# An added term ahead of each reciprocal: linear attention and spectral mixing on one core

## Chip, cores and metric

The kernel runs on one core of a Trainium2 chip. The metric is the device time of one execution in microseconds. The kernel before has a median of 419.33 us over three runs (418.85, 419.33 and 419.35).

## What is computed

The inputs are q, k and v of shape (8, 8, 576, 64) and the weights w_r, w_i (64, 512, 512) and w_ch (512, 512), all in float32. Cut to what matters:

```python
q_p, k_p = phi(q), phi(k)                      # phi(x) = max(x, 0) + 1 for x > 0, exp(x) below
kv  = einsum('bhsd,bhse->bhde', k_p, v)
z   = sum(k_p, axis=2)
num = einsum('bhsd,bhde->bhse', q_p, kv)
den = einsum('bhsd,bhd->bhs', q_p, z)[..., None] + 1e-06
x   = (num / den), heads side by side          # (8, 576, 512)
X   = rfft(x, axis=1); the first 64 modes are mixed over d by w_r + i w_i; y = irfft
u   = x + y
out = u + max(u @ w_ch, 0)
```

Each denominator is a sum of 64 products of features, and the reference adds 1e-6 to it. The kernel before divides by the sum alone.

## The kernel before, in words

The work is in three stages, and the order of nearly every instruction on every engine is written out by hand: `pin` (line 98) keeps an instruction at its place in the program.

**Attention stage (lines 436 to 475).** A loop over the 8 batches. For each batch q, k and v are loaded two batches ahead by DMAs issued on POOL's queue (`load`, L185; they go from float32 to float16, and each kind has two buffers, so a load waits until the batch two before has been used). ACT takes exponents (`exps`, L205 and L208) and DVE makes the features of them (`features`, L220, L226, and the copy of v into vpad, L232). PE transposes q into a PSUM tile qTp (`turn_q`, L242), ACT copies it out (L249). PE sums k and v into kvp (`sum_kv`, L262); v is padded with a column of ones, so that a 65th column holds z; ACT copies that into kv_sb (L274).

Then `form_x` (lines 279 to 304) runs over 5 tiles of rows, four of 128 and a tail of 64. PE multiplies into a PSUM tile num of two banks (`num_matmuls`, L156): for each of 8 heads 64 columns of numerator and one of denominator. DVE takes the reciprocal of the 8 denominators of each row straight from PSUM into rd (L295) and multiplies (L298), which leaves float16 rows x16, or x16t for the tail. The tiles qTp, kvp, num and xp share three PSUM buffers under the tag "big", so PE can be at most three such tiles ahead.

Between the tiles PE transforms the batch before to frequencies (`transform`, xf, L421 and L426; ACT scales the result into xsp, L433 and L434), and puts the one before that in its place as input of the weights' products (`place_x`, xp, L389 and L400; DVE and ACT copy it into xt_c, L409 and L410). On DVE the features of batch b+1 stand ahead of `form_x` of batch b. PE, DVE and ACT each go through this order; what is ahead in an engine's order holds up what is behind.

**Product stage (`mode_pair`, lines 532 to 557).** The 64 modes are handled as 32 pairs. A pair's weights are two DMAs of 1 MB written (`w_load`, L109, one for w_r and one for w_i), also on POOL's queue. Five pairs are loaded during the attention stage, and behind them w_ch (L600). From pair 5 on there are two buffers, so that the load of pair p+2 is issued when the products of pair p (L502, tile P) have read theirs; pair 5 takes the buffer of pair 0. In each pair DVE prepares the next input xz (L512), and DVE or ACT copies P out (L517, L519); PE sorts the result into yt (L525).

Into the gaps of this stage a work list is spread, so many items per pair. Its first items are `attention_rows` (lines 762 to 792): the rows of attention are computed a second time, now in float32 for the final sum. PE multiplies qT by kv_diag into banks nw (L773, four banks in turn). For even batches the reciprocals rd of the attention stage are used again; for odd batches, whose rows lie on other partitions, DVE takes the reciprocals anew, 4 per row and half tile, into rdw (L784). DVE multiplies (L786). Later items add the inverse transform to these rows and multiply by w_ch.

**Tail.** After the last load, in pieces (L121), the last modes, the inverse transform, the rectifier and the stores (L951, L957) follow.

The lines that matter here:

```python
        nv = num[orow, :, 0:260].rearrange("p o (c n) -> p o c n", c=4)
        rden = rd_all[b][orow, jj]
        pin(nc.vector.reciprocal(out=rden, in_=nv[:, :, :, 64]))
```

Of the kernel before, what the change touches and what calls it, by code (L numbers as in the profile page):

```python
# [33 lines left out]
def kernel(  # L34
# [10 lines left out]
    nc = tc.nc  # L45
# [52 lines left out]
    pin = tc.keep_in_program_order  # L98
# [45 lines left out]
    def rows_of(jj: int, base: int = 0):  # L144

        if jj < NJJ:
            return slice(base + jj, base + 512, NJJ)
        return slice(512, S) if base == 0 else slice(0, base)

    def num_matmuls(num, orow, qT, kv_sb, cols, pinned=False):  # L150
        for hpp in range(2):
            for h2 in range(2):
                for hpo in range(2):
                    rows = slice(hpo * 64, hpo * 64 + 64)
                    c0 = (hpp * 2 + h2) * 65
                    mm = nc.tensor.matmul(  # L156
                        num[hpo][orow, c0 : c0 + 65], qT[rows, hpp, h2, cols], kv_sb[rows, hpp, h2, :]
                    )
                    if pinned:
                        pin(mm)  # L160
        return [n[orow, 0:260].rearrange("p (c n) -> p c n", c=4) for n in num]

    def q_view(t):
        return t.rearrange("p (c t s) -> p c t s", c=2, t=2)
# [114 lines left out]
    def form_x(b, jj):  # L279
        if jj == 0:  # L280
            x16s[b] = (
                sA.tile([128, 2 * NJ * Dh * 2], F16, tag="x16", bufs=2, name=f"x16_{b}")[
                    :, 0 : NJJ * D
                ].rearrange("p (j d) -> p j d", j=NJJ),
                sA.tile([128, D], F16, tag="x16t", bufs=2, name=f"x16t_{b}"),
            )
        tail = jj == NJJ
        orow = HALVES[b % 2] if tail else slice(0, 128)
        num = psA.tile([128, 2, 512], F32, tag="big", bufs=3, name=f"num{b}_{jj}")
        num_matmuls(  # L290
            [num[:, o] for o in range(2)], orow, q_view(qT_all[b]), kv_all[b], rows_of(jj), True
        )
        nv = num[orow, :, 0:260].rearrange("p o (c n) -> p o c n", c=4)
        rden = rd_all[b][orow, jj]
        pin(nc.vector.reciprocal(out=rden, in_=nv[:, :, :, 64]))  # L295
        dst = x16s[b][1][orow, :] if tail else x16s[b][0][:, jj, :]
        pin(
            nc.vector.tensor_tensor(  # L298
                out=dst.rearrange("p (o c d) -> p o c d", o=2, c=4),
                in0=nv[:, :, :, 0:64],  # L300
                in1=rden.unsqueeze(3).broadcast_to([64 if tail else 128, 2, 4, Dh]),
                op=ALU.mult,
            )
        )
# [139 lines left out]
    for b in range(B):  # L444
        if b + 2 < B:
            load(b + 2)
            if b % 2 == 1:
                w_next()
        turn_q(b, 0)
        turn_q(b, 1)  # L450
        if b == 0:
            fold_table()
        sum_kv(b)
        if b + 1 < B:
            for _ in features(b + 1):
                pass
        if b + 2 < B:
            exps(b + 2)
        for jj in range(NJJ + 1):
            form_x(b, jj)  # L460
            if b == 0 and jj == 0:
                make_place()
            if b > 1 and jj == 1:
                place_x(b - 2)
            if b > 0 and jj in (2, 3):
                transform(b - 1, jj - 2)
        if b > 0:
            transform(b - 1, 2)
            transform(b - 1, 3)
# [204 lines left out]
    def x_of(t: int):  # L674
        if t < B * NJJ:
            return x_main[t // NJJ][:, t % NJJ, :]
        i = t - B * NJJ
        return x_tail[i // 2][:, i % 2, :]
# [10 lines left out]
    def bank(name: str, shape=(128, D), dtype=F32):  # L689
        return psB.tile(list(shape), dtype, tag="bank", bufs=4, name=name)  # L690
# [64 lines left out]
    def parts_of(t: int):  # L755
        if t < B * NJJ:
            b, jj = divmod(t, NJJ)
            return [(b, jj, slice(0, 128))]
        p = t - B * NJJ
        return [(2 * p + h, NJJ, HALVES[h]) for h in range(2)]  # L760

    def attention_rows(t: int):

        num = [bank(f"nw{t}_{c}") for c in range(2)]
        x = x_of(t)
        for b, jj, orow in parts_of(t):
            qT = q_view(qT_all[b])
            rd = rd_all[b][orow, jj].rearrange("p o (c t) -> p c t o", c=2)
            xv = x[orow].rearrange("p (o c t d) -> p c t o d", o=2, c=2, t=2)
            for c in range(2):  # L770
                for h2 in range(2):
                    pin(
                        nc.tensor.matmul(  # L773
                            num[c][orow, h2 * 130 : h2 * 130 + 130],
                            qT[:, c, h2, rows_of(jj, BASE[b % 2])],
                            kv_diag[:, b, c, h2].rearrange("p o n -> p (o n)"),
                        )
                    )
            for c in range(2):
                nv = num[c][orow, 0:260].rearrange("p (t o n) -> p t o n", t=2, o=2)  # L780
                rden = rd[:, c]
                if b % 2 == 1:
                    rden = sW.tile([128, 2, 2], F32, tag="rdw", bufs=4, name=f"rdw{t}_{c}")[orow]
                    pin(nc.vector.reciprocal(out=rden, in_=nv[:, :, :, 64]))  # L784
                pin(
                    nc.vector.tensor_tensor(  # L786
                        out=xv[:, c],
                        in0=nv[:, :, :, 0:64],
                        in1=rden.unsqueeze(3).broadcast_to([orow.stop - orow.start, 2, 2, Dh]),
                        op=ALU.mult,  # L790
                    )
                )
# [231 lines left out]
    def first_rows(n: int):  # L1024
# [8 lines left out]

    rows_work = [inverse_rows, row_sets] + [lambda i=i: row_set(i) for i in range(1 + N_LEAD)]
    work[:0] = [lambda t=t: attention_rows(t) for t in tiles[:8]] + rows_work + [
        lambda t=t: attention_rows(t) for t in tiles[8:]
    ]
    share(
# [98 lines left out]
    def sums_of(n: int, tiles_of):  # L1137
        channels(n, tiles_of)
        add_inverse(n, 1, tiles_of)
        for i in tiles_of:  # L1140
# [6 lines left out]
            out=x_of(0), in0=accs[0][:, 0], scalar=0.0, in1=x_of(0), op0=ALU.max, op1=ALU.add  # L1147
# [51 lines left out]
```

## Time and profile before

| | |
|---|---|
| Median of three runs | 419.33 us |
| Profiled execution | 418.91 us |
| Its span, first to last instruction | 417.2 us |
| PE, DVE, ACT, POOL busy | 292.3, 240.1, 152.7, 65.0 us |
| DMA moved | 92.86 MB, of it 81.54 MB issued on POOL's queue |
| Reciprocals L295 | 40, 198 ns in the median, from 25.5 to 104.9 us |
| Multiplies L298 | 40, 691 ns, from 25.8 to 105.1 us |
| Reciprocals L784 | 40, 172 ns, from 146.5 to 229.2 us |
| First product P starts | 114.75 us |
| Last piece of weights read by PE | 385.7 us |

All times within the execution are microseconds from the start of the span. A line of a timeline reads: start, duration, engine, line of the code, operation, output tile, input tile with their shapes, count, and in brackets how long the engine had been idle before it and what ended that. In the page's part 2 a digit is the busy share of one fortieth of the span (10.4 us), in tenths. A table of stages has for each stretch its length, the busy time of PE, PE's weight loads, DVE, ACT and POOL with the number of instructions, then the granted clock of PE, the DMA engines' share and GB/s. A line of DMA issues has the size and the microseconds from issue to landing.

### The profile page before, as it was taken

Reading aid. Unit: us, or ns where it says so; the run is one execution under the profiler, and the core shown is the slowest. Engines: PE = TensorE matmul, PEld = TensorE weight load, DVE = VectorE, ACT = ScalarE, POOL = GpSimd, SP = SyncE. Lnnn points to the kernel's source line nnn. Section 1 sums busy time; section 2 is a strip of 40 time slices with the busy share of each in tenths; the row PEclk is TensorE's granted clock in tenths of the full one; section 3 lists DMA queues with packets and bytes.
Section 4 is the critical chain, followed back from the end, with each engine's and each line's share of the span. In section 5 each row is a group of like instructions: output and inputs, shape, how many; then the busy total and the mean of one; then the engine's idle time right before and its main releaser. Section 6 shows DMA issues by size and latency. Waiting matters only on the chain.

```text
span 417.2 us, 6991 instructions
## 1 busy us (share of the span) xinstructions
PE 292.3 (70%) x2890; PEld 158.1 (38%) x2890; DVE 240.1 (58%) x533; ACT 152.7 (37%) x226; POOL 65.0 (16%) x115
## 2 busy tenths in 40 slices
PE   0279998999674355444435686978786887999993
PEld 0167776777421122212222232424332322453431
DVE  3779899695447474355536453564545354532795
ACT  4667787855200001000000233334342432331682
POOL 6232424200020111111111111111111111130200
PEclk9999999579755655566665589899998888899998
DMA  8999999999999999999999999999999999999698
GB/s 217 211 211 214 210 222 203 221 222 213 217 217 212 220 209 222 218 211 222 211 220 217 212 222 209 220 218 213 222 209 220 217 214 222 209 217 186 210 401 346
DMA packets 16998, 92.86 MB, mean 223 GB/s; under 512 B 2503, under 2 KB 3224, under 8 KB 12808
## 3 DMA queue, kind: packets, MB, share of 16 engines
q0 software_dynamic: 13088, 81.54, 94.0%
q1 hardware_dynamic: 3878, 10.90, 6.9%
q8 instruction: 22, 0.36, 0.3%
q14 instruction: 10, 0.07, 0.0%
HBM read 163.66 MB, written 9.44 MB: 415 GB/s over the span
## 4 chain that ended last, share of the span: by engine, by line
DMA 58%; PE 22%; DVE 9%; ACT 4%; issue 3%; POOL 3%; ACTq 0%; POOLq 0%
DMA w<-in_moe_w_i_dram 52%; DMA k<-in_k_dram 7%; PE P L502 5%; PE kvp L262 4%; DVE x_main L969 4%; DVE x L298 2%; PE qTp L242 2%; PE xp L389 2%; POOL w L109 2%; PE xf L421 1%; PE zl L489 1%; PE z L862 1%; ACT qT L249 1%; PE num L156 1%; PE acc L896 1%
## 5 line engine op out<-in xcount | busy, mean ns | idle before, releaser
L502 PE MATMUL P<-w,xz 128*32 128x512 bf16 x496 | 49.5, 540 | 70.8 <-DMA w<-in_moe_w_i_dram 68.5
L109 POOL DMA_DIRECT2D w<-in_moe_w_r_dram x31 | 17.3, 560 | 249.6 <-PE P L502 245.1
L519 ACT CAST ys<-P 128x512 f16<-128x512 f32 x15 | 8.8, 586 | 120.4 <-PE P L502 120.4
L502 PEld LDWEIGHTS <-xz 128*32 128x32 bf16 x496 | 13.6, 116 | 91.9 <-DMA w<-in_moe_w_i_dram 55.8
L517 DVE CAST ys<-P 128x512 f16<-128x512 f32 x17 | 11.8, 692 | 55.3 <-PE P L502 55.3
L842 PE MATMUL eps<-wch,xTw 128*128 128x512 f16 x144 | 41.1, 413 | 0.0
L825 ACT CAST x16w<-x_main 128x512 f16<-128x512 f32 x32 | 19.8, 618 | 37.0 <-DVE x_main L823 37.0
L823 DVE TENSOR_TENSOR x_main<-ya,x_main 128x512 f32<-128x512 f32 x32 | 22.0, 689 | 19.0 <-PE ya L819 18.8
L262 PE MATMUL kvp<-vpad,ke 32*128 32x130 f16 x576 | 23.8, 261 | 8.3 <-ACT qT L249 8.3
L773 PE MATMUL nw<-kv_diag,qT 128*128 128x130 f16 (+1 forms) x160 | 24.3, 294 | 6.6 <-DVE x_tail L786 3.2
L850 ACT CAST E<-eps 128x512 f16<-128x512 f32 (+1 forms) x40 | 21.2, 540 | 20.1 <-PE eps L842 20.1
L262 PEld LDWEIGHTS <-ke 32*128 32x128 f16 x576 | 21.9, 115 | 9.8 <-issue 9.2
L512 DVE COPY xz<-xt_c 64x256 bf16<-64x256 bf16 x62 | 22.9, 369 | 2.2 <-PE P L502 1.4
L298 DVE TENSOR_TENSOR x<-num,rd 128x512 f16<-128x512 f32 x32 | 22.1, 691 | 1.1
L242 PE MATMUL qTp<-id,qe 128*128 128x128 f16 x144 | 14.2, 277 | 11.4 <-DVE qe L226 9.7
L773 PEld LDWEIGHTS <-qT 128*128 128x128 f16 (+1 forms) x160 | 14.5, 134 | 20.0 <-issue 11.5
L834 DVE COPY xTw<-xTp 128x512 f16<-128x512 f16 x36 | 15.0, 416 | 10.5 <-PE xTp L832 10.4
L156 PE MATMUL num<-kv_sb,qT 64*128 64x65 f16 (+1 forms) x320 | 16.3, 218 | 6.3 <-DVE x L298 3.9
L249 ACT COPY qT<-qTp 128x1152 f16<-128x1152 f16 x16 | 19.6, 1289 | 2.1 <-PE qTp L242 2.0
L786 DVE TENSOR_TENSOR x_main<-nw,rd 128x256 f32<-128x256 f32 x32 | 11.2, 415 | 15.1 <-PE nw L773 15.1
L208 ACT ACTIVATE ke<-k 128x2304 f16<-128x2304 f16 x8 | 16.9, 2116 | 3.2 <-DMA k<-in_k_dram 3.2
L842 PEld LDWEIGHTS <-xTw 128*128 128x128 f16 x144 | 13.6, 106 | 11.6 <-issue 4.5
(153 smaller groups left out, 526.6 us busy)
## 6 DMA issues: line engine op xcount, KB each, us to landing
w<-in_moe_w_r_dram POOLq DMA_DIRECT2D x31, 1024.0 KB, 12.3
w<-in_moe_w_i_dram POOLq DMA_DIRECT2D x31, 1024.0 KB, 16.6
out_dram<-x_main SPq DMA_DIRECT2D x14, 512.0 KB, 3.4
v<-in_v_dram POOLq DMA_DIRECT2D x8, 576.0 KB, 14.2
q<-in_q_dram POOLq DMA_DIRECT2D x7, 576.0 KB, 12.5
k<-in_k_dram POOLq DMA_DIRECT2D x6, 576.0 KB, 12.5
q<-in_q_dram SPq DMA_DIRECT2D x2, 576.0 KB, 4.5
w<-in_moe_w_r_dram POOLq DMA_DIRECT2D x2, 512.0 KB, 11.2
```

The costliest lines, as they stand in the source:

```text
L109: nc.gpsimd.dma_start(out=w_in[p][half::2], in_=two.rearrange("g (r dc) e -> (g r) dc e", dc=NDW))
L156: mm = nc.tensor.matmul(num[hpo][orow, c0 : c0 + 65], qT[rows, hpp, h2, cols], kv_sb[rows, hpp, h2, :])
L242: nc.tensor.transpose(qT_ps[:, j], phi["q", b][:, c, j].rearrange("p o d -> p (o d)"), id16,)
L249: nc.scalar.copy(out=qT[:, :, c * NJ : (c + 1) * NJ], in_=qT_ps.rearrange("p j x -> p x j"))
L262: nc.tensor.matmul(kv_ps[:, h2, 0:130], phi["k", b][r0 : r0 + 32, j // NJ, j % NJ].rearrange("p o d -> p (o d)"), vp[r0 : r0 + 32, :, j, 0 ...
L298: nc.vector.tensor_tensor(out=dst.rearrange("p (o c d) -> p o c d", o=2, c=4), in0=nv[:, :, :, 0:64], in1=rden.unsqueeze(3).broadcast_to([ ...
L502: nc.tensor.matmul(P[c : c + n, :], x, w[:, dc, :], start=(dc < NDC), stop=(dc >= n_dc - NDC), tile_position=(0, c), skip_group_check=True,)
L512: pin(nc.vector.tensor_copy(out=xz[p % 2][HALVES[h], :, h, :], in_=src))
L773: nc.tensor.matmul(num[c][orow, h2 * 130 : h2 * 130 + 130], qT[:, c, h2, rows_of(jj, BASE[b % 2])], kv_diag[:, b, c, h2].rearrange("p o n ...
L823: pin(nc.vector.tensor_tensor(out=x, in0=acc, in1=x, op=ALU.add))
L842: nc.tensor.matmul(e_ps, xT[:, c, :], wch16[:, c, :], start=(c == 0), stop=(c == NDC - 1))
L850: pin(nc.scalar.copy(out=dst, in_=e_ps[:, cols]))
```

## The change

Ahead of each of the two reciprocals a `tensor_scalar_add` on the vector engine reads the denominators from PSUM, adds 1e-6 and writes them to the tile of the reciprocals; the reciprocal then works in place on that tile.

```diff
@@ form_x
         rden = rd_all[b][orow, jj]
-        pin(nc.vector.reciprocal(out=rden, in_=nv[:, :, :, 64]))
+        pin(nc.vector.tensor_scalar_add(out=rden, in0=nv[:, :, :, 64], scalar1=1e-6))
+        pin(nc.vector.reciprocal(out=rden, in_=rden))
@@ attention_rows
                 if b % 2 == 1:
                     rden = sW.tile([128, 2, 2], F32, tag="rdw", bufs=4, name=f"rdw{t}_{c}")[orow]
-                    pin(nc.vector.reciprocal(out=rden, in_=nv[:, :, :, 64]))
+                    pin(nc.vector.tensor_scalar_add(out=rden, in0=nv[:, :, :, 64], scalar1=1e-6))
+                    pin(nc.vector.reciprocal(out=rden, in_=rden))
```

## The prediction

> **What bounds the kernel now.** I read the page first. Its 40 slices show the DMA engines full from the first slice to near the end, and DVE at 7 to 9 tenths in the first ten slices; the chain gives DMA 58%.
>
> ```profile
> DVE  3779899695447474355536453564545354532795
> DMA  8999999999999999999999999999999999999698
> DMA 58%; PE 22%; DVE 9%; ACT 4%; issue 3%; POOL 3%; ACTq 0%; POOLq 0%
> ```
>
> So for 386 of 417 us the kernel is a stream of loads, and an edit to DVE counts only if it makes the stream run dry. The chain in order of time says where that can be. Up to 114.75 it mixes PE, DVE, ACT and one load; from 133 to 385 it is one load after another. The hand-over is between: the first product P (L502) waits for the last of the attention stage, and the load of pair 5 waits for that product. The POOL queue's timeline and the issues with their landing times, each asked for a stretch of its own, price it:
>
> ```profile
> 87.25 0.78 POOL L600 DMA_DIRECT2D wch<-in_moe_w_ch_dram  x1 [4.33 <-DMA w<-in_moe_w_r_dram]
> 116.95 0.52 POOL L109 DMA_DIRECT2D w<-in_moe_w_r_dram  x1 [28.92 <-PE P L502]
> ```
> ```profile
> wch<-in_moe_w_ch_dram POOLq DMA_DIRECT2D x1, 512.0 KB, 36.2
> ```
> ```profile
> w<-in_moe_w_r_dram POOLq DMA_DIRECT2D x1, 1024.0 KB, 11.4
> ```
>
> POOL stood idle 28.92 us for P. wch lands at 87.25+36.2 = 123.5. Pair 5's first half, issued at 116.95, lands at 128.35, 4.85 later, and 4.85 per half is the pace of all loads (their landings are spaced so). The stream was therefore not dry: there is a **cushion**. The packets say how much: the first of the 16 DMA engines is through with wch at about 121.25, the last at about 123.2, and the last small loads (row L1122) take about 1.1 us from issue to first packet; I use 1.3. An issue by 121.25-1.3 = 119.95 leaves no engine idle (cushion 3.0 us); by 123.2-1.3 = 121.9 the slowest engine alone is still covered (4.9 us). I take **3.0**, since past it engines stand idle, and keep 4.9 for the range.
>
> **What the change does to DVE.** The instruction order of the changed kernel has 80 more instructions, all on DVE: 40 adds at L295 and 40 at L784 (the latter for odd batches). Each add takes the wait for PE over; the reciprocal then waits for the add, as the multiply waits for the reciprocal. Nothing else moves; no DMA is added. The DVE timeline shows the unit into which an add goes:
>
> ```profile
> 28.49 0.20 DVE L295 RECIPROCAL rd<-num 128x8 f32<-128x8 f32 x1
> 28.72 0.69 DVE L298 TENSOR_TENSOR x<-num,rd 128x512 f16<-128x512 f32 x1
> 29.33 0.20 DVE L295 RECIPROCAL rd<-num 128x8 f32<-128x8 f32 x1
> ```
>
> From a reciprocal to the multiply that needs it is 0.23 us: 0.20 and 0.03 of waiting. No add of this shape is in the trace. The nearest above is the TENSOR_SCALAR of L355, from PSUM, 128x64 in 0.215; below, a MEMSET of one column in 0.06. With the 0.03 the add costs 0.09 to 0.25; below nothing is excluded, as an instruction is put into a chain and none is taken out. I take **0.235**, the pitch of the reciprocal, the row that it is nearest to (same tile, same kind of wait). The reciprocal now reads SBUF and not PSUM: I leave it at 0.20, within 0.03 either way (L741, SBUF, 128x16: 0.178).
>
> [...]
>
> **The attention stage (25 to 106 us): 40 tiles, 5 per batch, 5 x 0.235 = 1.2 us per batch.** I walk along the DVE timeline and take off every idle gap before it.
> - Batches 0 to 2: DVE is 1.2 later after each, and gets back what it had idle before vpad (0.33 at 35.67, 0.92 at 46.30) and before xt_c (0.63 at 49.59), as far as PE isn't late too. PE is, since num has 3 buffers and waits for the multiply before the last two. Left: 0.9, 1.15, then 1.75.
> - Batches 3 and 4 (52.8 to 77): DVE has no gap. 2.9, then 4.1; PE, which waits for x there already, 3.6.
> - At 73.82 PE's transposes of batch 5 had waited 1.20 us for ACT, which stood behind the load of k that landed at 71.04. That load was queued 13.3 us, so its landing doesn't move when its issue comes 1.8 later. Left: 3.6-1.2 = 2.4; DVE's 2.61 idle before 79.51 comes down to the same.
> - Batch 5: PE is the slower, DVE's gaps of 0.63 and 0.32 are used: 2.8. Batch 6: DVE 4.0, PE 3.3, and DVE's idle 4.12 before 100.79 brings it down to PE's:
>
> ```profile
> 96.13 1.18 PE L242 MATMUL qTp<-id,qe 128*128 128x128 f16 x18
> ```
> ```profile
> 100.79 0.21 DVE L295 RECIPROCAL rd<-num 128x8 f32<-128x8 f32 x1 [4.12 <-PE num L156]
> 105.11 0.69 DVE L298 TENSOR_TENSOR x16t<-num,rd 64x512 f16<-64x512 f32 x1
> ```
> - Batch 7: 3.3+1.15 = **4.4** at x16t, for which PE's xf already waits 0.32; then a chain of PE, DVE and ACT with no slack to P at 114.75.
>
> So of 9.4 us of adds 4.4 reach P. The issue at 116.95 becomes 121.35: 4.4-3.0 = **1.4 us of dry stream**, and from there the stream is a fixed train (9.7 us a pair), with a tail of 31.5 us after 385.7 that nothing touches. At the cheap end of the add (0.09) the walk gives some 1.7, inside the cushion; at 0.25 some 4.7, and 1.7 over.
>
> Earlier loads are covered: q of batch 7 is issued at 65.47, behind DVE's features of batch 5, now near 68.4; the stream has v of batch 6 until 73.7, less some 2 us of landing. What queues behind it on POOL (k, v, then eight halves of w) has more. If this cover went, its loss would come earlier and the cushion at 117 would grow by it.
>
> **The product stage (146 to 229 us): 40 adds more, 0.2 each, 8 us, costed at nothing.** P waits for its load, and after P the next issue has a whole pair in flight:
>
> ```profile
> 220.58 1.90 PE L502 MATMUL P<-w,xz 128*32 128x512 bf16 x16 [5.59 <-DMA w<-in_moe_w_i_dram]
> 230.27 1.90 PE L502 MATMUL P<-w,xz 128*32 128x512 bf16 x16 [2.15 <-DMA w<-in_moe_w_i_dram]
> ```
>
> The tightest pair has 10 of the 40 adds (224 to 229.8): PE's nw matmuls wait for DVE's banks, so P at 230.27 may lose up to 2.1 of its 2.15 us. Were it late, the next issue would have some 7 us before the stream is dry. If all this cover were gone, it would be up to 8 us.
>
> **Sum.** 418.91 (profiled execution; span 417.2 and 1.7 around it) + 1.4 = 420.3. The three runs have median 419.33, 0.4 above it; I give the median's figure, 419.33 + 1.4 = **420.7**. Runs differ by 0.5 us, so about 0.2% (0.84 us) is what can be told from no change.
>
> **Rivals.**
> - *The cushion holds: no change.* Mechanism: DMA engines that run dry for a moment don't matter as long as the slowest isn't, so the cushion is 4.9 and not 3.0; it decides from a delay of 4.9 us on. For it: w lands when its last engine does, and 4.4 is under 4.9; a cheaper add, 0.15, gives 2.8. Against: the mean rate over 16 engines has nothing spare. Time: 419.3 (419.0 to 420.1).
> - *PE loses clock: slower still.* The stages view:
>
> ```profile
> 60.00:70.00 10.00, 8.63 (x176) 6.87 (x175) 9.66 (x19) 7.80 (x11) 3.11 (x5) 1.00 1.01 199
> 70.00:80.00 10.00, 8.09 (x118) 6.82 (x117) 7.22 (x14) 7.29 (x11) 2.74 (x6) 0.59 1.13 216
> 90.00:95.00 5.00, 4.53 (x108) 3.69 (x100) 4.47 (x10) 1.87 (x6) 0.00 (x0) 1.00 0.99 210
> ```
> The third column from the end is the granted clock. It falls about 72, after PE waited for x several times at 68.8 to 71. A batch at low clock takes PE 12.9 us (73.82 to 86.72), at full clock 9.4 (86.72 to 96.13); DVE with the adds needs about 10.4. More waiting for x can drop the clock one batch sooner, at 12.9-10.4 = 2.5 us: 420.7+2.5 = 423.2. Against: at 59 to 62 a wait of 0.59 didn't drop it. [...]
> - *Faster.* A clock gained in batch 5 would make up delay, but the stream has no gap to give; 419.33 less over 0.84 has no mechanism beyond a shift of that clock.
> - *It doesn't do what it says* is excluded: the adds stand in the order.
>
> **Numbers.** Forecast (over the cushion by 0.9 to 3) 0.47; cushion holds 0.37; clock lost 0.11; faster 0.05. So slower 0.58, same 0.37, faster 0.05. The range runs from 419.0, within the holding case, to 423.3, the clock's case: some 0.17 is left out.
>
> **What would show it.** After: DVE's L295 twice per tile at a pitch near 0.235; P first at about 119.2 and not 114.75; POOL's issue at about 121.3; its landing at about 129.8, and not 128.35, with wch still at 123.5; product pairs again 9.7 apart; 31.5 us after the last load. The cushion's case shows P late and the landing unchanged. The clock's case shows four xf matmuls at 0.62 instead of 0.41 between 58 and 72 or 95 and 106. I am wrong in kind if k's landing moves or a product pair exceeds 9.7.

## The result, and the profile after

The changed kernel takes 423.74 us in the median of 10 runs (420.07 to 425.55), the kernel before 419.01 us (418.83 to 419.35, 10 runs beside them): a ratio of 1.009 (of the means), interval 1.0061 to 1.012. It is slower by 4.7 us where 1.4 was forecast. The ten times are not one cluster: four lie at 420.1 to 420.3, six at 423.7 to 425.6, and before shows nothing of the kind. The profiled execution is one of the upper six: 424.23 us with a span of 422.5, against 418.91 and 417.2. Ratios here are taken without executions over 1.5% above the fastest of the same kernel; that matters for three experiments, and stands there.

First the page of the changed kernel: DVE, the granted clock, the DMA engines and their rate in 40 slices, which are now 10.6 us each, then the engines' shares of the chain.

```profile
DVE  4769889896544784466555653463527262622794
PEclk9999998588665555555665589798989696899997
DMA  8999999999999999999999999999999999998697
GB/s 216 212 210 216 209 215 188 214 209 218 220 169 220 220 208 218 220 217 209 219 221 206 219 223 214 211 220 218 208 221 219 216 213 220 217 208 164 240 402 304
DMA 49%; PE 27%; DVE 12%; ACT 4%; issue 3%; POOL 3%; ACTq 0%; DVEq 0%; POOLq 0%
```

The busy shares of the DMA engines look as full as before, but their rate does not. The same row of before's page:

```profile
GB/s 217 211 211 214 210 222 203 221 222 213 217 217 212 220 209 222 218 211 222 211 220 217 212 222 209 220 218 213 222 209 220 217 214 222 209 217 186 210 401 346
```

Before had no slice under 203 GB/s among the first 36, now slice 7 (63 to 74 us) has 188 and slice 12 (116 to 127 us) has 169. The stream has run dry twice. The chain says the same from the other side: DMA has lost 9 points, PE has gained 5 and DVE 3.

Next DVE's timeline of the changed kernel, for the same unit as in the prediction:

```profile
28.92 0.15 DVE L295 TENSOR_SCALAR rd<-num 128x8 f32<-128x8 f32 x1
29.11 0.20 DVE L296 RECIPROCAL rd<-rd 128x8 f32<-128x8 f32 x1
29.34 0.69 DVE L299 TENSOR_TENSOR x<-num,rd 128x512 f16<-128x512 f32 x1
```

The add takes 0.154 us in the median (0.146 to 0.170) and its successor starts 0.19 after it. The reciprocal that now reads SBUF takes 203 ns, against 198 from PSUM. Then the hand-over, from the POOL queue's timeline and PE's:

```profile
70.54 0.71 POOL L185 DMA_DIRECT2D q<-in_q_dram  x1 [8.23 <-ACT kv_sb L274]
...
88.69 0.78 POOL L601 DMA_DIRECT2D wch<-in_moe_w_ch_dram  x1 [4.31 <-DMA w<-in_moe_w_r_dram]
123.50 0.52 POOL L109 DMA_DIRECT2D w<-in_moe_w_r_dram  x1 [34.04 <-PE P L503]
```
```profile
121.30 1.90 PE L503 MATMUL P<-w,xz 128*32 128x512 bf16 x16 [2.25 <-ACT xt_c L411]
```

P starts at 121.30 instead of 114.75, 6.55 us late, and POOL issues pair 5 at 123.50 instead of 116.95. The issues with their landing times, of wch and of pair 5's first half:

```profile
wch<-in_moe_w_ch_dram POOLq DMA_DIRECT2D x1, 512.0 KB, 36.3
```
```profile
w<-in_moe_w_r_dram POOLq DMA_DIRECT2D x1, 1024.0 KB, 7.8
```

Pair 5's half lands at 123.50 + 7.8 = 131.3, not 128.35: 2.95 late. wch lands at 124.99, not 123.45, so 1.5 of the 2.95 are older. They come from the first row of the POOL fence: q of batch 7 was issued at 70.54, not 65.47, and the rate of the stream fell (slice 7 above). The other 1.45 us are lost between 123 and 126.5.

Last, the granted clock by stages, third column from the end:

```profile
60.00:70.00 10.00, 9.74 (x177) 7.49 (x175) 8.65 (x21) 8.18 (x9) 0.89 (x2) 1.00 1.01 199
70.00:80.00 10.00, 9.05 (x112) 6.50 (x107) 9.56 (x23) 7.00 (x11) 6.09 (x9) 0.58 1.03 175
80.00:90.00 10.00, 9.79 (x158) 7.77 (x156) 7.94 (x19) 7.99 (x9) 1.86 (x3) 0.57 1.08 225
90.00:100.00 10.00, 9.14 (x163) 7.21 (x163) 9.56 (x21) 4.70 (x9) 0.00 (x0) 0.83 1.01 215
```

The 1.00 of the first row must be read with care: up to the first change that a trace records, 64.75 us here, this column and the page's digits show full clock, also where the matmuls tell of half. PE's transposes of a batch (L242, 18 of them) tell the clock by themselves: before's take 1.18 us at 96.13, where the stages grant 1.00, and 2.10 at 86.72, where they grant 0.50. PE's timelines of before and of the changed kernel, batch 3:

```profile
52.84 1.18 PE L242 MATMUL qTp<-id,qe 128*128 128x128 f16 x18
```
```profile
54.82 2.10 PE L242 MATMUL qTp<-id,qe 128*128 128x128 f16 x18
```

In the changed kernel the first rise is at 64.75; before it was at 51.4. Between 50 us and P, with the time before the first rise counted as half clock, the changed kernel's PE was at half clock for 44.0 us, before's for 23.8. Those 20 us are what the prediction did not have.

### The profile page after: what moved, and what is told of

The parts are those of the page before. It is cut to its first block, busy times and chain, and to the rows that moved or that the text cites. A ratio compares the mean times of both kernels' runs of the same rounds, so it can differ in the third digit from the quotient of the medians.

```text
span 422.5 us, 7071 instructions
## 1 busy us (share of the span) xinstructions
PE 301.8 (71%) x2890; PEld 163.5 (39%) x2890; DVE 253.0 (60%) x613; ACT 153.0 (36%) x226; POOL 65.0 (15%) x115
## 4 chain that ended last, share of the span: by engine, by line
DMA 49%; PE 27%; DVE 12%; ACT 4%; issue 3%; POOL 3%; ACTq 0%; DVEq 0%; POOLq 0%
DMA w<-in_moe_w_i_dram 46%; PE P L503 6%; PE kvp L262 4%; DVE x_main L971 4%; DMA k<-in_k_dram 3%; PE xp L390 2%; DVE x L299 2%; PE xf L422 2%; PE qTp L242 1%; ACT qT L249 1%; POOL w L109 1%; PE z L864 1%; PE num L156 1%; PE eps L844 1%; PE zl L490 1%
## 5 line engine op out<-in xcount | busy, mean ns | idle before, releaser
L503 PE MATMUL P<-w,xz 128*32 128x512 bf16 x496 | 48.6, 532 | 60.2 <-DMA w<-in_moe_w_i_dram 58.0
L844 PE MATMUL eps<-wch,xTw 128*128 128x512 f16 x144 | 42.2, 422 | 0.0
L774 PE MATMUL nw<-kv_diag,qT 128*128 128x130 f16 (+1 forms) x160 | 25.4, 302 | 13.0 <-DVE x_tail L788 3.7
L262 PE MATMUL kvp<-vpad,ke 32*128 32x130 f16 x576 | 25.2, 272 | 8.8 <-ACT qT L249 8.8
L262 PEld LDWEIGHTS <-ke 32*128 32x128 f16 x576 | 23.4, 121 | 10.3 <-issue 9.4
L242 PE MATMUL qTp<-id,qe 128*128 128x128 f16 x144 | 14.3, 277 | 10.3 <-DVE qe L226 9.6
L156 PE MATMUL num<-kv_sb,qT 64*128 64x65 f16 (+1 forms) x320 | 17.2, 227 | 5.9 <-DVE x L299 3.5
L109 POOL DMA_DIRECT2D w<-in_moe_w_i_dram x31 | 17.7, 571 | 3.6 <-DMA v<-in_v_dram 2.2
## 6 DMA issues: line engine op xcount, KB each, us to landing
w<-in_moe_w_r_dram POOLq DMA_DIRECT2D x31, 1024.0 KB, 12.6
v<-in_v_dram POOLq DMA_DIRECT2D x8, 576.0 KB, 12.6
```

The lines of the kernel that those rows point to most:

```text
L109: nc.gpsimd.dma_start(out=w_in[p][half::2], in_=two.rearrange("g (r dc) e -> (g r) dc e", dc=NDW))
L156: mm = nc.tensor.matmul(num[hpo][orow, c0 : c0 + 65], qT[rows, hpp, h2, cols], kv_sb[rows, hpp, h2, :])
L262: nc.tensor.matmul(kv_ps[:, h2, 0:130], phi["k", b][r0 : r0 + 32, j // NJ, j % NJ].rearrange("p o d -> p (o d)"), vp[r0 : r0 + 32, :, j, 0 ...
L503: nc.tensor.matmul(P[c : c + n, :], x, w[:, dc, :], start=(dc < NDC), stop=(dc >= n_dc - NDC), tile_position=(0, c), skip_group_check=True,)
L774: nc.tensor.matmul(num[c][orow, h2 * 130 : h2 * 130 + 130], qT[:, c, h2, rows_of(jj, BASE[b % 2])], kv_diag[:, b, c, h2].rearrange("p o n ...
L844: nc.tensor.matmul(e_ps, xT[:, c, :], wch16[:, c, :], start=(c == 0), stop=(c == NDC - 1))
```

## The experiments

Two theories stood after the comparison. **The walk's**: the adds in the attention stage delay P, what exceeds the cushion is lost, and the rest of the kernel follows. **The clock's**: the adds shift PE's clock, and most of the 6.55 us at P come from there. In the quoted expectations the walk's is theory A and the clock's theory C; the other letters are variants and rivals, explained where they stand. "Low" below is the time at half clock between 50 us and P, in the profiled execution.

| kernel | profiled, us | low | P | issue of pair 5 | its half lands | median, us |
|---|---|---|---|---|---|---|
| before | 418.91 | 23.8 | 114.75 | 116.95 | 128.35 | 419.01 |
| after | 424.23 | 44.0 | 121.30 | 123.50 | 131.3 | 423.74 |
| e1_attention_only | 419.21 | 15.3 | 115.87 | 117.54 | 128.6 | 422.63 |
| e2_product_only | 419.24 | 22.8 | 113.79 | 115.99 | 128.6 | 419.24 |
| e9_adds_batches_0_2 | 419.25 | 13.6 | 111.39 | 113.59 | 128.9 | 419.01 |
| e10_adds_batches_3_7 | 422.90 | 39.9 | 120.61 | 122.81 | 130.6 | 419.57 |
| e11_add_twice | 430.52 | 58.2 | 128.66 | 130.87 | 138.8 | 429.04 |
| e12_change_again | 425.54 | 41.5 | 122.23 | 124.43 | 132.4 | one run |
| e3_clock_primed | 424.38 | 43.9 | 120.88 | 122.84 | 130.7 | 421.23 |
| e4_term_on_tensor_engine | 435.29 | 79.8 | 133.20 | 135.40 | 143.2 | 428.74 |
| e7_clock_held | 427.53 | 17.1 | 124.17 | 126.37 | 134.3 | 426.50 |
| e8_one_copy_to_act | 419.26 | 23.6 | 114.52 | 116.72 | 128.6 | 419.35 |

The two with a shorter cushion, e5 and e6, load in another order and stand in their own paragraph.

### One half of the change at a time

e1_attention_only has the first hunk of the change alone, e2_product_only the second.

> The adds stand only in the attention stage (40 of 80); the odd batches' second reciprocals in the product stage are without the 1e-6. Theory A (late P, dry stream): all of the cost is here, so the time is that of the full change, in two groups near 420.2 and near 424.5 us, the first product P after 118 us, and the load of pair 5 issued at 120 or later. Rival B (the product stage's adds cost): near 419.0.

> The adds stand only in the product stage (40 of 80); the attention stage divides without the 1e-6. Theory A: 419.0 us within 0.3, P at 114 to 116, product pairs 9.7 us apart. Rival B: 420 or more, with pairs over 9.7 us apart between 146 and 229 us.

e2: 11 runs of 419.10 to 419.64 beside before, ratio 1.0 (0.9991 to 1.0009). The 40 adds of the product stage cost nothing by themselves. e1: 419.08 to 425.02 over 12 runs, ratio 1.0067 (1.0037 to 1.0096). So the cost is in the attention stage: e1's interval includes the change's 1.009. The two groups that I expected of e1 were not there: its runs spread, and three lie at 419.1 to 419.2. The profiled execution is one of these three, with P at 115.87 where I expected it after 118: PE's timeline and the stages.

```profile
115.87 1.37 PE L503 MATMUL P<-w,xz 128*32 128x512 bf16 x16 [2.25 <-ACT xt_c L411]
```
```profile
70.00:80.00 10.00, 8.52 (x135) 6.50 (x131) 9.55 (x23) 7.21 (x8) 4.78 (x9) 0.66 1.12 214
80.00:90.00 10.00, 8.91 (x152) 7.00 (x148) 9.45 (x23) 8.11 (x12) 2.10 (x3) 0.83 1.07 226
90.00:100.00 10.00, 9.02 (x203) 7.42 (x199) 8.09 (x20) 4.82 (x10) 0.00 (x0) 1.00 1.00 214
```

It has every add of the attention stage and yet P only 1.12 us later than before, because its clock is back earlier (0.83 and 1.00 where the changed kernel has 0.57 and 0.83). The batches show where the changed kernel is later. DVE's last multiply of batches 2 and 3 (x16t), in the changed kernel and then in e1, from DVE's timelines:

```profile
53.99 0.68 DVE L299 TENSOR_TENSOR x16t<-num,rd 64x512 f16<-64x512 f32 x1
67.06 0.69 DVE L299 TENSOR_TENSOR x16t<-num,rd 64x512 f16<-64x512 f32 x1
```
```profile
54.01 0.68 DVE L299 TENSOR_TENSOR x16t<-num,rd 64x512 f16<-64x512 f32 x1
64.83 0.69 DVE L299 TENSOR_TENSOR x16t<-num,rd 64x512 f16<-64x512 f32 x1
```

Batch 3 takes 13.07 us in the changed kernel, where PE is at half clock until 64.75, and 10.82 in e1, where it is so for 3.4 us only. Batch 5 takes 12.84 and 11.11, batches 4 and 6 take 10.94 in both. These two batches at half clock are 4.0 of the 5.4 us by which the changed kernel's P is later than e1's, with the same instructions ahead of P.

### Which batches

The add is kept in part of the batches; the others leave out the 1e-6 in the attention stage.

```diff
-        pin(nc.vector.reciprocal(out=rden, in_=nv[:, :, :, 64]))
+        den = nv[:, :, :, 64]
+        if b < 3:          # e10: b > 2
+            pin(nc.vector.tensor_scalar_add(out=rden, in0=den, scalar1=1e-6))
+            den = rden
+        pin(nc.vector.reciprocal(out=rden, in_=den))
```

> The change, with the attention stage's adds in batches 0 to 2 alone (15 of 40; the other batches divide without the 1e-6 there). Theory C2: the clock rises in batch 2 (44 to 52 us) without the adds, and adds ahead of that point can push the rise to batch 3 (65 us), which is what makes the upper group. Then two groups stay here: P at 114 to 115 or near 117 to 118, times 419.2 and 420 to 422. Theory A alone (the sum of DVE's delays along the walk): of 15 adds, 1.4 us at most are left at batch 3, so P at 115 to 116 and one group at 419.2.

> The change, with the attention stage's adds in batches 3 to 7 alone (25 of 40). Theory C2: the rise stays at 44 to 52 us as in the kernel before, there is no upper group, P at 115 to 117, 419.0 to 420.3 in all runs. Theory A alone: 25 adds cost more than 15, P at 116 to 118, and the times lie above those of the adds in batches 0 to 2.

e9: 418.89 to 419.29 over 11 runs, ratio 0.9995 (0.9986 to 1.0003). That the early adds push back the first rise of the clock, and that this is the loss, fell with it. Its profiled execution even has the earliest P of all, 111.39: PE, later by the early adds, waits for x only 0.2 us between 50 and 106 us (before 1.6), and every batch from 3 on is transposed at full clock. PE's timeline of e9:

```profile
64.16 1.18 PE L242 MATMUL qTp<-id,qe 128*128 128x128 f16 x18
74.27 1.18 PE L242 MATMUL qTp<-id,qe 128*128 128x128 f16 x18
```

e10: 419.29 to 425.68 over 12 runs, median 419.57, ratio 1.0022 (1.0002 to 1.0043; one run left out). Eight runs pay less than 1 us; four pay 2 to 6 us, which theory C2 had excluded. Its profiled execution is one of those: the clock rises at 51.2, falls at 61.4 for 17.1 us, and again at 95.6 for 20.5 us. PE waits for x 3.0 us there. So the spread needs the adds of batches 3 to 7 only, where DVE has the longer work and PE waits for it.

### The add twice

```diff
         pin(nc.vector.tensor_scalar_add(out=rden, in0=nv[:, :, :, 64], scalar1=1e-6))
+        pin(nc.vector.tensor_scalar_add(out=rden, in0=rden, scalar1=0.0))
```

> The change, with a second add (of 0, in place on the tile of the reciprocals) behind each add of the attention stage: 40 instructions more, 0.15 to 0.19 us each, 0.9 us per batch. Theory A: past the cushion each us by which P is later is a us of time, so the lower group comes 2 to 4 us above that of the change, 422 to 424, and the upper group 426 to 429; DVE is then the bound in nearly each batch. If the clock alone decides: the groups stay at 420.2 and 424.5.

428.32 to 430.52 in four runs, ratio 1.0239 (1.022 to 1.0258), more than expected. P is at 128.66. The DMA engines' strip for 112 to 132 us (40 pieces of 0.5 us, in tenths) of e10's profiled execution, and then of e11's:

```profile
DMA  9797999799999679999852009531979919499493
```
```profile
DMA  9919799394997939768899974210000000000000
```

In e10, where pair 5 is issued at 122.81, the engines drain from 122, stand at 0 for two pieces from 123, and are full again from 126 or so. In e11 they are empty from 125.5 to the end of the strip, since the issue comes only at 130.87. This is the dry stream of the prediction, seen directly, in two sizes.

### A smaller cushion

The load of w_ch, 512 KB, moves behind the loads of pairs 5 and 6, in before (e5) and in after (e6). At the stream's pace (4.85 us for 1 MB) the cushion shrinks by 2.4 us.

```diff
-    tc.keep_in_program_order(
-        nc.gpsimd.dma_start(out=wch16, in_=moe_w_ch.rearrange("(c p) j -> p c j", p=128))
-    )
...
         mode_pair(p)
+        if p == 1:
+            w_get(n_early), w_get(n_early + 1)
+            pin(
+                nc.gpsimd.dma_start(out=wch16, in_=moe_w_ch.rearrange("(c p) j -> p c j", p=128))
+            )
```

> The kernel before, with the load of w_ch moved behind the loads of pairs 5 and 6: the stream has 2.6 us less queued when P ends. Theory A with E (a cushion of 3.0 to 4.9 us, which in the kernel before hides what PE's clock does to P from run to run): between 0.4 and 2.3 us of cushion are left, so 419.0 where P is at 114 to 115 and up to 422 where P comes late, a spread of over 1 us between runs instead of 0.5. Rival F (there is no such cushion, the late weights cost by themselves): 419.0 in all runs.

> The changed kernel with the load of w_ch moved in the same way. Theory A with E: the cushion is gone, and each run is 2.6 us slower than the group it would have been in: 422.5 to 428. Rival F: as the changed kernel, 420 to 425.5.

e5: 418.85 to 419.76 in ten runs, ratio 1.0002 (0.9993 to 1.0011). These ten stay inside even this cushion, so a P that comes more than some 1.3 us late from run to run, which before would merely hide, is not seen in them. (Of before's 73 runs beside the experiments 68 took at most 419.53 us and five 419.91 to 420.31; none of the five was profiled.) e6: 421.76, 421.82, 428.25 and 428.69; the ratio 1.0062 (1.0044 to 1.0081) is of the lower two. Set beside the change's two groups, these are 1.6 and some 3.8 us later, where 2.4 each would follow. The profiled executions show the dry stream: e6 (P at 116.57, pair 5 issued at 118.49) moves 188 GB/s from 112 to 122 us, and e5 (P at 113.80, issued at 116.00) 216. But pair 5's half lands only 0.6 us later in e6 than in e5, and the rest of the 2.4 us between these two executions comes in small pieces later. The cushion is real; its size doesn't follow from these two runs.

### The clock, taken by itself

e3 has 26 unused matmuls of 128x512 in batch 0, e7 six at the head of each batch's sums (both on the changed kernel); e4 has before's instructions on DVE, and PE adds the term with a matmul of 4 columns behind each bank (the matmuls ahead of it then stay open as one sum per bank).

```diff
# e3
             fold_table()
+            spin(14)
...
+        if b == 0 and jj > 1:
+            spin(4)
# e7
+            if pair == 0:
+                spin(kv_ps[:, 0], 6)
# e4
+        for n in num:
+            add_eps(n[orow, 64:260:65])
```

> The full change, and 26 matmuls of 128x512 more whose results nobody reads, put where PE waits in batch 0 (14 behind the table's matmuls, 4 behind the numerators of each of the last three tiles), to keep PE's clock up from about 20 us on. Theory C (a late rise of PE's clock is the part above the forecast): the rise comes at 20 to 40 us and not at 51 or 65, P comes 2 us or more before the 121.3 us of the profiled execution, the issue for q of batch 7 before 70.5, and the time loses its upper group: 419.0 to 420.5 in all runs. Rival D (DVE's adds alone do it, the clock is no matter): two groups as with the change, 420.2 and 424.5.

> The changed kernel with 6 matmuls of 128x512 more per batch, at the head of the first kvp tile, behind the transposes; nobody reads them. Theory C (the clock's rise decides the group): the clock is up by 35 us and is not seen at a half for a whole batch after that; the dummies take 1.3 us per batch at full clock, so a batch takes 10.7 to 11.1 us, P at 114 to 118, and all runs lie between 419.0 and 420.0. Rival D (the adds alone): P at 121 and later, 423 to 428, since PE has more to do.

> The 1e-6 is added by PE and not by DVE: one matmul of 4 columns (ones times 1e-6/128) accumulates into the four denominators of each bank ahead of the reciprocal, twice a tile, in both stages. DVE's order is that of before. Theory A, by which DVE is what makes P late: PE gets some 10 small matmuls per batch, 0.05 to 0.1 us each, so 0.5 to 1 us per batch where PE's clock is low and it is the bound, and little where DVE is the bound: P at 116 to 118, inside the cushion, 419.0 to 419.6 us. If PE is as much the bound as DVE: P at 119 to 121 and the time as with the change.

e3: 420.44 to 424.38, ratio 1.0038 (1.0025 to 1.0051). The clock rose at 18.8 us and fell again at 35.8 to 63.1 and at 76.8 to 104.1; P at 120.88 missed what I expected. This early rise wasn't kept. e7: 426.29 to 428.37, ratio 1.0184 (1.0165 to 1.0202). The unused matmuls took 1.5 to 2.7 us a batch where I had allowed 1.3, PE and DVE waited for each other in turn (4.2 and 3.8 us between 50 and 106 us), and P was at 124.17 with little low clock (17.1 us). The times are those that rival D gave; but with so much work added to PE, e7 doesn't decide between the theories. So no experiment held the clock up without adding work. e4: 419.19 to 435.29 over 12 runs; without the seven above 425.5 the ratio is 1.001 (0.9999 to 1.0021), so in those five the term on PE costs next to nothing, or what it costs stays inside the cushion. The seven fit neither outcome that I had named. The profiled execution is among them, and I use it for one reading only, PE's timeline:

```profile
133.20 1.90 PE L519 MATMUL P<-w,xz 128*32 128x512 bf16 x16 [2.26 <-ACT xt_c L427]
```

From batch 1 on every batch's transposes take 2.10 there, the first rise comes at 128.4, and P is 18.45 us late with DVE's work unchanged. How this splits between the clock and the added matmuls at half clock was not measured.

### The change once more

e12_change_again is the changed kernel, unedited, for a second profile.

> The changed kernel, unchanged, for a second profile of the same program. Theory C: if its time is near 420.2, the clock rose at 44 to 54 us, P came at 115.5 to 117.5 and w of pair 5 was issued before 120; if near 424, the rise is at 60 us or later and P at 120 or later, as in the first profile.

425.54 us, upper group, but the clock rose at 52.5 and not past 60, as I had expected of that group. It was low again from 62.7 to 79.8 and from 96.9 to 117.3. PE's timeline of e12, where the row at 54.09 is batch 3's transposes and the next batch 4's:

```profile
54.09 1.18 PE L242 MATMUL qTp<-id,qe 128*128 128x128 f16 x18
65.31 2.10 PE L242 MATMUL qTp<-id,qe 128*128 128x128 f16 x18
```

So the first rise alone doesn't set the group. The sum of low clock goes with it in these two: 41.5 us here, 44.0 in the first profile.

### A version that keeps the term

In the changed kernel DVE's half of the copy xp to xt_c goes to ACT, which has room.

```diff
-        pin(nc.vector.tensor_copy(out=xt_v[:, 0:h, :, b, :], in_=psf[:, 0:h]))
+        pin(nc.scalar.copy(out=xt_v[:, 0:h, :, b, :], in_=psf[:, 0:h]))
```

> The changed kernel, with DVE's half of the copy of xp into xt_c (0.69 us per batch) moved to ACT. Theory A with C: DVE gets back 0.69 of its 0.95 us per batch, so P comes some 2 us earlier than with the change at the same clock, but the clock's two groups stay: 419.0 to 419.5 and 422 to 423.5. If ACT becomes the bound (it stands behind the loads of q and k): no gain, 420 to 425.5.

419.16 to 419.49 in ten runs and 421.23 in one, ratio 1.0006 (0.9996 to 1.0015); P at 114.52. The upper group that theory A with C left standing is gone but for the one run. This has the 1e-6 everywhere and can't be told from before. No version was found that beats before.

## Why the prediction was right, and where it fell short

The sign held. The ratio on the 419.33 that the prediction started from gives 423.1, just inside its upper end of 423.3; the raw median, 423.74, is just past it, and the forecast itself, 420.7, describes only the lower four runs. That the range held is in part luck: its upper end was taken from a rival that had been given 0.11.

**Right: where most of it is paid.** The adds of the product stage cost nothing (e2), and the late issue of pair 5 behind P costs what exceeds a cushion (e10, e11). Two further losses, one earlier and one later, stand at the end of this section.

**The cushion: 3.0, to 4.9 foreseen; about 3.7 by the runs.** A half issued on a dry stream lands 7.8 to 8.0 us later (after, e10, e11, e12), and one on a full stream lands at 128.35 to 128.9. The last harmless issue is thus about 128.5 - 7.85 = 120.65, and 120.65 - 116.95 = 3.7, an estimate good to some 0.4.

**The add: 0.235 foreseen, 0.19 measured.** The pitch of the nearest row was too dear by a quarter. The reciprocal was left at 0.20 from SBUF, and it is 0.203. That is 5 ns more than the 198 from PSUM before.

**The delay of P by the adds alone: 4.4 foreseen, 2.9 or 4.3 by two ways of counting.** Four executions have all adds of the attention stage and no other work ahead of P: low 15.3, P 115.87 (e1); 19.1, 116.57 (e6); 41.5, 122.23 (e12); 44.0, 121.30 (after). Between the first two and the last two P moves 5.5 us for 25.6 us of low clock, 0.22 per us. At before's 23.8 that straight line through four points gives about 117.6, 2.9 after before's P. By batches it is more. Before had batch 5 at half clock, as the changed kernel had; what the changed kernel had beyond that is batch 3, which cost 13.07 - 10.82 = 2.25, and 6.55 - 2.25 leaves about 4.3. The walk with 0.19 would give 4.4 x 0.19/0.235 = 3.6. So the adds alone end near the end of the cushion, 0.8 us short of it or 0.6 past it; the second is nearer to the lower four runs.

**The step that failed: the clock.** The walk took the adds along before's pattern of clock, and "PE loses clock one batch sooner" was a rival with 0.11 and 2.5 us. In the first profile one batch more did run at half clock, by a late rise and not an earlier fall, for the 2.25 us above; in e12 two falls, at 62.7 and 96.9, gave batches of 12.6 and 12.4. By the straight line 20 us more at half clock at 0.22 come to 4.4, against the 3.65 of P's 6.55 that the adds then leave. By either count the clock is at least most of the 2.85 us by which 6.55 exceeds the cushion. The sign that the prediction had named for this case is there, four xf matmuls at 0.62 and not 0.41 between 58 and 72 us, in the changed kernel's PE timeline:

```profile
64.07 0.62 PE L422 MATMUL xf<-fwd_sb,x 128*128 128x128 f16 x4
```

The rival's figure, 423.2, is near the median; its chance was far too small. What spoke for it stood in the prediction: DVE needs some 10.4 us a batch (10.9 in e1) and PE 9.4 at full clock, so PE waits for x where it runs fast, 3.0 to 3.6 us between 50 and 106 us in e1, e10 and e12 against 1.6 before. But it is 0.9 in the changed kernel's first profile, and 0.9 in e11. Where DVE has no add (e9) or gives a copy away (e8) in batches 3 to 7, the time stays at 419 but for one run of e8. In before, e2, e3, e5, e8, e10 and e12 each fall of 17 us and more that began between 60 and 100 us did so within 2 us of a wait of PE for x of 0.4 to 1.05 us. But the falls in the changed kernel at 71.6 and in e11 at 60.0 had no wait over 0.2 us in the 5 us before them, and in e1 a wait of 1.04 that ended at 71.8 was followed by a fall of only 6.8 us, in e6 two waits of 0.79 by falls of 3.4. So waiting for x goes with many of the falls; that it causes them is not shown, and it is not the whole condition. What decides in a run between one step of low clock and five stays open.

**"Earlier loads are covered" failed with it.** The issue of q of batch 7 was put at 68.4 and came at 70.54; the stream lost 1.5 us there, and wch moved. I had named a pair above 9.7 us as a sign of being wrong in kind: one spacing of two pairs' products is 10.24 right after the hand-over, the rest up to 234 us are 9.7 to 10.0. Later ones scatter in both kernels (8.3 to 11.7 before, 8.4 to 12.0 now).

**What does not add up.** From pair 5's landing, 2.95 late, to the end of the span, 5.3 late, 2.4 us come in small pieces: 0.5 in the next pair, 1.3 more to the last product, 0.6 behind it. e10, e11 and e12 have 1.4 to 2.9 us of this kind above their issue's delay past the cushion. I have no cause for it. Nor is there a profile of the lower group of the changed kernel itself; that it has the clock of e1 or e6 is inferred, and why it still costs 1.2 us more than before is not shown. Nor was the clock ever set by itself: its share rests on executions that differ in it by chance.

## What to carry to other kernels

Small work added to an engine that is even with TensorE may be paid twice: once in its own time, here up to 0.95 us a batch (five adds of 0.19), and once in each further batch in which TensorE runs at half its clock, here some 2 us (13.07 against 10.82 in batch 3 and 12.84 against 11.11 in batch 5, the changed kernel against e1). That the adds bring on the half clock was not shown. Walk such a change with both clocks and weigh the slow one, above all where the clock already falls in the profile. Where the time is a train of loads, find the last harmless issue first, since a delay short of it was hidden here: in e1's profiled execution pair 5 was issued 0.59 us later than before, its half landed at 128.6, and the time was 419.21 us. Where an engine with room could take a like piece off the loaded one (e8), the cost was gone in ten of eleven runs.

## What the hardware showed

- In the clock records of before and of the changed kernel each stretch between two changes, from the first rise on, is 3.41 us or a multiple of it (up to 88.75 us). Over the profiled executions a fall that began before 105 us lasted one or two steps or five to eight (17.1 to 27.3 us); from P on, falls lasted up to 99 us (e6). The longest wait of PE at a long fall before 105 us was 2.14 us (e3, at 35.8), most were 0.4 to 1.05, and the fall of the changed kernel at 71.6 had none over 0.2 in the 5 us before it.
- A busy PE was not always granted full clock: in e4's profiled execution, one of the seven above 425.5 us, PE was busy for 49.2 of the 50 us from 60 to 110, by the stages, and each batch's transposes took 2.10; the first rise came at 128.4 us.
- On DVE, in medians, the add of 128x8 from PSUM took 154 ns (changed kernel, L295), the reciprocal 198 ns from PSUM (before, L295) and 203 from SBUF (changed kernel, L296). With 128x4 in the product stage the add took 150 ns (L785), the reciprocal 172 from PSUM (before, L784) and 178 from SBUF (changed kernel, L786).
